# Batch 0's attention scores in twelve groups, more room for their weights, and a reordered middle stretch, in a fused attention and ReGLU feed-forward kernel

## The chip, the cores and the metric

The kernel runs on one core of a Trainium2 chip. The core has five engines, each with its own queue: TensorE (PE in the profile, with its weight loads as PEld), VectorE (DVE), ScalarE (ACT), GpSimd (POOL) and SyncE (SP). SP only issues DMA here; ACT and POOL issue some too. The metric is the device time of one execution in microseconds, taken as the median of three runs. Before the change that is 373.52 us (373.01 to 375.04).

## The reference

```python
def _attn_ref(q, k, v):
    B, H, S, D = q.shape                 # 8, 8, 576, 64
    block = 64
    scores = (1 / np.sqrt(D)) * np.matmul(q, k.transpose(0, 1, 3, 2))
    pos = np.arange(S)
    mask = pos[:, None] // block >= pos[None, :] // block
    scores = np.where(mask, scores, -1e9)
    attn = np.exp(scores - np.max(scores, axis=-1, keepdims=True))
    attn = attn / (np.sum(attn, axis=-1, keepdims=True) + 1e-09)
    return np.matmul(attn, v)

def _moe_ref(x, w_gate, w_val, w_out):   # x: 4608 x 512; weights 512 x 1536 and 1536 x 512
    gate = np.maximum(x @ w_gate, 0.0)
    val = x @ w_val
    return gate * val @ w_out
```

The attention output of batch b, 576 tokens by 512 features (8 heads of 64), is x for the feed-forward network (FFN). Inputs and output are float32; the kernel multiplies in bf16.

## The kernel before

**Units of work.** A *round* r is one batch and one pair of heads: b, hp = divmod(r, 4), so rounds 0 to 3 are batch 0 and rounds 4 to 7 are batch 1. The first 512 tokens of a batch are four chunks of 128 and the last 64 are its tail. Scores are computed transposed, keys on partitions and queries along columns; of chunk c only the queries from chunk c on are needed, so a round has three groups per head: chunk 0 (512 columns), chunks 1 and 3 (384 + 128) and chunk 2 (256). The two heads of a pair lie on partitions 0 to 63 and 64 to 127 and run on PE side by side. ACT takes the exp from PSUM into SBUF (`exp`, L466). `corners` and `corner` (L531 to L539) zero the 64 x 64 blocks that the mask excludes. `head_av` (L586) multiplies the exponentials with v, which has a column of ones, so that the row sum comes with it; `normalise` (L544) divides into `xnat`; `to_xT_pe` (L640) transposes `xnat` back through PE into `xT`, the input of the FFN, with head pair hp as its chunk c = hp.

**Layout of batch 0 and 1.** These batches are loaded with four tokens to a partition, token = 4p + j. `pe_mains` (L344) transposes a head pair of q and k on PE and copies both out of PSUM into `qTm` and `kTm`, and the copy brings the columns back to token order.

**FFN.** `ffn_gen` (L679) is a generator. For batch j it makes twelve groups f of 128 hidden columns. A group is 8 matmuls of 512 columns: 4 for the gate, one for each chunk c of x, and 4 for the value. ACT takes the ReLU (L704), DVE multiplies (L709) into `hT`. Then come four output blocks of 128 tokens, 12 matmuls each (L724), DVE copies them to `ob` (L736, three buffers), and `put` stores them one block late; for j = 0 POOL issues the store (L671), otherwise ACT. For j < 2 the groups 0 and 1 are made together, and their steps are sorted so that the four matmuls with c = 3, which need the last head pair, come last. `ffn(n)` runs n more matmuls, to the end of the group begun; `ffn_parts(n)` runs n parts of 4 matmuls.

**PSUM.** Banks 0 to 5 are given out by `take`: the least recently used bank or pair of banks. Banks 6 and 7 (`AV`) are for `head_av`, and for `pe_mains` and `sort_v` where the call names them. `sort_v` (L293) brings v of batch 1 into chunk order with matmuls.

**Where the exponentials go.** `attnT` has two buffers, for even and odd rounds. Round 2 has its first 1024 columns in the space of `v_p` (`attnE`), which is used for v of batch 1 later.

**Order.** All five queues run in the order in which the program is written out (L785 to L982): an instruction waits on its engine for whatever it needs, and everything behind it waits too. DMA loads go through a ring of ten staging buffers; POOL casts them to bf16, which frees the buffer for a later load.

The stretch for batch 0 is L793 to L843: transposes, scores in two calls a round (`scores_1` and `scores_2`), weighted sums, first FFN parts. The weights of the gate and the value come in six halves of 256 hidden columns (`load_w_half`) for each third i of the hidden columns. The stretch for batch 1 is L864 to L924; its attention is laid between FFN matmuls of batch 0. `tails.cast` (L888) is ten casts on POOL for the tails of batches 0 and 1.

Of the kernel before, what the change touches and what calls it, by code (L numbers as in the profile page):

```python
# [17 lines left out]
def kernel(  # L18
# [10 lines left out]
    nc = tc.nc  # L29
# [19 lines left out]
    AV = 6  # L49
    taken = [0] * 6  # L50
# [30 lines left out]

    attnE = v_p.rearrange("p j n -> p (j n)")

    def attn(r, lo, hi):

        if r == 2 and hi <= 1024:
            return attnE.rearrange("p (g n) -> p g n", g=2)[:, :, lo:hi]
        return attnT[r % 2][:, :, lo:hi]

    zeros = consts.tile([128, 128], BF, name="zeros")  # L90
# [89 lines left out]
    class Early:  # L180
# [163 lines left out]
        def pe_mains(self, hp, evac, out=None):  # L344
            out = out or pair()
            for t in range(2):
                tp = as_bf(out[:, t, :])[:, 0:512]
                src = self.half(t, hp // 2)
                lo = 128 * (hp % 2)
                for j in range(4):  # L350
                    nc.tensor.transpose(  # L351
                        tp[:, 128 * j : 128 * j + 128], src[:, j, lo : lo + 128], ident
                    )
                evac[t](
                    (qTm, kTm)[t][self.b % 2][:, :, hp, :].rearrange(
                        "p c (n j) -> p c n j", j=4
                    ),
                    tp.rearrange("p (j c n) -> p c n j", j=4, c=4),
                )

        def pe_tails(self, evac):

# [80 lines left out]
    def cast_w(sts, eng):  # L443
        for dst, st in sts:
            eng(dst, st)


    def scores(b, hp, sc, pieces):
        for pos, c, main in pieces:
            for hh in range(2):  # L450
                ps = slice(64 * hh, 64 * hh + 64)
                n = 512 - 128 * c if main else 64
                o = sc[:, hh, pos : pos + n]
                if main:
                    o = o.rearrange("p (c n) -> p c n", n=128)
                nc.tensor.matmul(  # L456
                    o,
                    kTm[b % 2][ps, c, hp, :],
                    qTm[b % 2][ps, c:4, hp, :] if main else qTt[b % 2][ps, hp, :],
                    start=True,  # L460
                    stop=True,
                )
        return sc

    def exp(out, sc):
        nc.scalar.activation(out, sc, AF.Exp, scale=scale)  # L466

    def scores_1(r):

        b, hp = divmod(r, 4)  # L470
        sc = scores(b, hp, banks[:, 0:2] if r % 2 == 0 else banks[:, 2:4], [(0, 0, True)])
        exp(attn(r, 0, 512), sc)
        sc = scores(
            b, hp, banks[:, 2:4] if r % 2 == 0 else banks[:, 0:2],
            [(0, 1, True), (384, 3, True)],
        )
        exp(attn(r, 512, 1024), sc)

    def scores_2(r):
        b, hp = divmod(r, 4)  # L480
        sc = scores(b, hp, banks[:, 0:2] if r % 2 == 0 else banks[:, 2:4], [(0, 2, True)])
        exp(attn(r, 1024, 1280), sc[:, :, 0:256])

    def scores_all(r, tails=True):

# [193 lines left out]
    def ffn_gen():  # L679

        for j in range(B + 1):
# [4 lines left out]
            for fs in groups:  # L686
# [2 lines left out]
                steps = [(f, t, c) for f in fs for t in range(2) for c in range(4)]  # L689
                if len(fs) > 1:  # L690

                    steps.sort(key=lambda step: (step[2] == 3, step[1]))
                for n, (f, t, c) in enumerate(steps):
                    i, fo = f // 4, 128 * (f % 4)
                    nc.tensor.matmul(  # L695
# [87 lines left out]
    with tc.manual_schedule(engines={E.PE, E.DVE, E.Activation, E.Pool, E.SP}):  # L783
# [5 lines left out]
        for h0 in (0, 2, 4, 6):  # L789
            e0.load_v(h0, 2)  # L790
        w_0 = [load_w_half(0, g) for g in range(2)]
        w_1 = [load_w_half(1, g) for g in range(2)]
        constants(0, nc.vector)  # L793
        constants_tail(0, nc.vector)
        selection(nc.vector.memset, nc.vector.tensor_copy)
# [5 lines left out]
        constants_tail(1, nc.gpsimd)  # L801
        for h0 in (2, 4, 6):
            e0.cast_qk(h0, 2, (pool, pool))
        scores_1(0)
        e0.pe_mains(1, (dve, dve), banks[:, 4:6])
        scores_2(0)
        e0.pe_mains(2, (dve, dve), banks[:, 6:8])
        scores_1(1)
        corners(0, nc.gpsimd)
        e0.cast_v(0, 2, pool)  # L810
        scores_2(1)
        e0.pe_mains(3, (dve, dve), banks[:, 4:6])
        corners(1, nc.gpsimd)
        e0.cast_v(2, 2, pool)
        scores_1(2)
        head_to_xnat(0, 0)
        head_to_xnat(0, 1)
        scores_2(2)
        e0.cast_v(4, 2, pool)
        for c in range(4):  # L820
            corner(2, c, nc.gpsimd)
        head_to_xnat(1, 0)
        head_to_xnat(1, 1)
        scores_1(3)
        to_xT_pe(0, (dve,), banks[:, 4])
        e0.cast_v(6, 2, pool)
        cast_w(w_0[0], pool)
        head_to_xnat(2, 0)
        head_to_xnat(2, 1)
        scores_2(3)  # L830
        to_xT_pe(1, (act,), banks[:, 5])
        for c in range(4):
            corner(3, c, nc.vector)
        cast_w(w_0[1], pool)
        to_xT_pe(2, (act,), banks[:, 4])
        head_to_xnat(3, 0)
        head_to_xnat(3, 1)
        taken[:] = [1, 1, 2, 2, 3, 3]
        ffn_parts(3)
        to_xT_pe(3, (act, dve), banks[:, 5])  # L840
        for w in w_1:
            cast_w(w, pool)
        cast_w(load_w_half(2, 0), pool)  # L843
        e1 = Early(1)
        es = (e0, e1)
        e1.load_qk(0, 4)
        w_2 = load_w_half(2, 1)
        e1.load_v_packed(0)

        ffn(20)  # L850
        w_out = [load_w_out(i) for i in range(3)]
        e1.load_qk(4, 4)
# [8 lines left out]
        cast_w(w_out[2], pool)  # L861
        e1.cast_qk(4, 4, (pool, pool))
        e1.cast_v_packed(4, pool)
        ffn(40)  # L864
        e1.pe_mains(0, (dve, act), banks[:, AV : AV + 2])
        ffn(8)
        e1.pe_mains(1, (dve, act), banks[:, AV : AV + 2])
        scores_all(4, False)
        corners(4, nc.vector)
        ffn(16)  # L870
        e1.sort_v(0, (dve, act), banks[:, AV : AV + 2])
        scores_all(5, False)
# [138 lines left out]
```

## Time and profile before

| | us |
|---|---|
| median of three runs | 373.52 |
| lowest, highest | 373.01, 375.04 |
| the profiled execution's own time | 374.13 |
| its span, first to last instruction | 372.3 |
| PE busy | 355.8 (96%) |
| ACT busy | 170.8 (46%) |
| DVE busy | 165.8 (45%) |
| POOL busy | 117.0 (31%) |

The profile is one execution. A busy share is an average over stretches with different limits; in this kernel the two stretches named above have the most idle time of PE. The granted TensorE clock is 1.00 on the page throughout. The end of a matmul is modelled: one of 512 columns is shown with 379 ns on average while one starts every 216 ns, so the distance between starts is what counts. A timeline row gives the start in us, the length, the engine and line, the operation with the tile it writes and those it reads, and how many instructions are merged in it; in brackets stands how long the engine was idle before it, and what ended that.

### The profile page before, as it was taken

The numbers are of one execution on the slowest core, as the hardware profiler recorded it, in microseconds if no ns is written. First come the engines' busy times: TensorE is split into PE (matmuls) and PEld (weight loads), VectorE is DVE, ScalarE is ACT, GpSimd is POOL, SyncE is SP. The second block draws the span as 40 slices with busy tenths as digits, with TensorE's granted clock in tenths as the row PEclk, the third lists the DMA queues.
The fourth block names the chain that finished last, engine by engine and source line by source line (L and its number), as shares of the span: only waits on it lengthen the run. The fifth ranks groups of instructions, "written<-read, shape, count | busy, mean of one in ns | idle before, by whom it ended". The sixth has DMA issues, their size and how long they took to land.

```text
span 372.3 us, 7468 instructions
## 1 busy us (share of the span) xinstructions
PE 355.8 (96%) x2954; PEld 188.0 (50%) x2993; DVE 165.8 (45%) x329; ACT 170.8 (46%) x269; POOL 117.0 (31%) x161
## 2 busy tenths in 40 slices
PE   7799997899999999999999999999999999999995
PEld 3544554555565555555555555555554544444443
DVE  5744443447565644354434443544344433423432
ACT  4833725656665564365436543654365403302310
POOL 4766778165879302920193004000000000000000
PEclk9999999999999999999999999999999999999999
DMA  8999999969999983997299829063301130020013
GB/s 253 264 349 351 378 195 341 162 158 262 206 168 180 101 149 75 161 119 136 74 173 108 137 75 150 19 132 64 102 16 18 44 102 1 2 85 28 2 35 106
DMA packets 140915, 51.02 MB, mean 137 GB/s; under 512 B 119504, under 2 KB 135120, under 8 KB 140880
## 3 DMA queue, kind: packets, MB, share of 16 engines
q1 hardware_dynamic: 79472, 34.29, 40.3%
q0 software_dynamic: 56704, 8.13, 37.5%
q10 hardware_dynamic: 4704, 8.13, 6.2%
q8 instruction: 23, 0.38, 0.5%
q14 instruction: 12, 0.10, 0.1%
HBM read 37.75 MB, written 9.44 MB: 127 GB/s over the span
## 4 chain that ended last, share of the span: by engine, by line
PE 90%; ACT 4%; DMA 2%; issue 1%; DVE 1%; SPq 0%; POOL 0%; ACTq 0%
PE banks L695 50%; PE banks L724 24%; PE banks L600 7%; PE banks L456 6%; ACT attnT L466 3%; DMA stage<-in_k_dram 2%; PE banks L567 1%; PE banks L351 1%; PE banks L645 1%; PE banks L301 1%; SPq L193 0%; DVE xnat L549 0%; ACT v_p L466 0%; ACT xT L652 0%; ACT kTt L375 0%
## 5 line engine op out<-in xcount | busy, mean ns | idle before, releaser
L466 ACT ACTIVATE attnT<-banks 128x1024 bf16<-128x1024 f32 (+1 forms) x122 | 87.9, 805 | 61.3 <-PE banks L456 55.7
L704 ACT ACTIVATE gate_sb<-banks 128x512 bf16<-128x512 f32 x108 | 64.9, 603 | 101.9 <-PE banks L695 101.6
L709 DVE TENSOR_TENSOR hT<-gate_sb,banks 128x512 bf16<-128x512 bf16 x108 | 74.0, 688 | 78.1 <-PE banks L695 72.5
L695 PE MATMUL banks<-xT,wg 128*128 128x512 bf16 x364 | 97.4, 379 | 2.5 <-DVE xT L650 0.8
L695 PE MATMUL banks<-xT,wv 128*128 128x512 bf16 x378 | 98.2, 379 | 0.4
L724 PE MATMUL banks<-wo,hT 128*128 128x512 bf16 (+1 forms) x433 | 96.0, 373 | 0.7 <-issue 0.2
L695 PEld LDWEIGHTS <-wv 128*128 128x128 bf16 x432 | 42.3, 98 | 51.0
L724 PEld LDWEIGHTS <-hT 128*128 128x128 bf16 x444 | 42.4, 98 | 46.5 <-issue 0.2
L695 PEld LDWEIGHTS <-wg 128*128 128x128 bf16 x432 | 40.5, 98 | 46.5 <-issue 1.9
L736 DVE COPY ob<-banks 128x512 f32<-128x512 f32 (+1 forms) x37 | 25.1, 677 | 56.9 <-PE banks L724 55.3
L399 POOL DMA_DIRECT2D v_bf<-in_v_dram x16 | 14.3, 906 | 73.3 <-PE banks L600 73.3
L600 PE MATMUL banks<-v_bf,attnT 128*128 128x65 bf16 x816 | 34.9, 194 | 0.6 <-DVE recip L548 0.3
L600 PEld LDWEIGHTS <-attnT 128*128 128x128 bf16 x816 | 30.3, 98 | 8.4 <-issue 0.6
L549 DVE TENSOR_TENSOR xnat<-banks,recip 128x640 bf16<-128x640 f32 (+2 forms) x36 | 25.9, 721 | 1.2
L456 PE MATMUL banks<-qTm,kTm 64*128 64x512 bf16 (+3 forms) x256 | 24.2, 299 | 1.1 <-ACT attnT L466 0.9
L456 PEld LDWEIGHTS <-kTm 64*128 64x128 bf16 x512 | 16.9, 94 | 11.1 <-issue 2.3
L548 DVE RECIPROCAL recip<-banks 128x10 f32<-128x10 f32 (+3 forms) x38 | 8.0, 209 | 29.7 <-PE banks L600 27.1
L535 DVE MEMSET attnT<- 64x192 uint32 x28 | 6.1, 218 | 24.3 <-ACT attnT L466 21.6
L399 POOL DMA_DIRECT2D k_bf<-in_k_dram x16 | 14.1, 906 | 0.7 <-DMA v_bf<-in_v_dram 0.5
L399 POOL DMA_DIRECT2D q_bf<-in_q_dram x16 | 14.3, 932 | 0.0
L695 PE MATMUL banks<-xTt,wg 128*128 128x512 bf16 x48 | 12.3, 379 | 0.1
L695 PE MATMUL banks<-xTt,wv 128*128 128x512 bf16 x46 | 12.1, 379 | 0.1
(97 smaller groups left out, 200.1 us busy)
## 6 DMA issues: line engine op xcount, KB each, us to landing
out_dram<-ob ACTq DMA_DIRECT2D x28, 256.0 KB, 2.2
stage<-in_moe_w_gate_dram SPq DMA_DIRECT2D x6, 512.0 KB, 9.0
stage<-in_moe_w_val_dram SPq DMA_DIRECT2D x6, 512.0 KB, 8.9
stage<-in_q_dram SPq DMA_DIRECT2D x6, 512.0 KB, 7.5
stage<-in_k_dram SPq DMA_DIRECT2D x6, 512.0 KB, 8.6
stage<-in_moe_w_out_dram SPq DMA_DIRECT2D x6, 512.0 KB, 9.8
stage<-in_v_dram SPq DMA_DIRECT2D x8, 256.0 KB, 7.0
q_bf<-in_q_dram POOLq DMA_DIRECT2D x16, 128.0 KB, 5.9
```

The source lines that it names most:

```text
L399: nc.gpsimd.dma_start(dst, src[b, :, 128 * c : 128 * c + n, :].rearrange("h p d -> p h d"),)
L456: nc.tensor.matmul(o, kTm[b % 2][ps, c, hp, :], qTm[b % 2][ps, c:4, hp, :] if main else qTt[b % 2][ps, hp, :], start=True, stop=True,)
L466: nc.scalar.activation(out, sc, AF.Exp, scale=scale)
L535: eng.memset(three[:, :, :, 0:64], 0.0)
L548: nc.vector.reciprocal(recip, av[:, :, :, 64])
L549: nc.vector.tensor_tensor(out=out, in0=av[:, :, :, 0:64], in1=recip.to_broadcast([rows, heads, n, 64]), op=AX.mult,)
L600: nc.tensor.matmul(av[:, 0, p, :], w, vb[:, c, h, :], start=(p == 0), stop=(c == p), skip_group_check=True,)
L695: nc.tensor.matmul(out[f][:, t, :], (wg, wv)[t][i][:, c, fo : fo + 128], x[:, c, :], start=(c == 0), stop=(c == 3),)
L704: nc.scalar.activation(gate[f], out[f][:, 0, :], AF.Relu)
L709: nc.vector.tensor_tensor(out=h, in0=gate[f], in1=out[f][:, 1, :], op=AX.mult)
L724: nc.tensor.matmul(ops[:, g, 0 : n1 - n0], hT[f][:, 128 * s : 128 * (s + 1)], wo[i][:, f % 4, n0:n1], start=(f == 0), stop=(f == 11),)
L736: nc.vector.tensor_copy(ob, ops[:, g, 0 : n1 - n0])
```

## The change

- **Twelve groups.** `scores_1` and `scores_2` give way to `scores_of(g)`: group g is the third i of round r, with r, i = divmod(g, 3). Groups take banks 0 and 1 or banks 2 and 3 in turn. Between two groups stand transposes, weighted sums or transposes of `xnat`.
- **Room for all rounds.** `attn` gives rounds 2 and 3 space of their own: the first 1024 columns in `v_p` and in the first third of `w_out`'s tile, the last 256 of each in the second third's. `w_out` is cast there later. Before, only round 2 had other space, for its first 1024 columns.
- **Queries as loaded.** For batch 0 the copy of q out of PSUM keeps the order (p, j), and the scores' matmul reads the columns with j innermost, through the new function `queries`; a step from j to j + 1 is 512 elements.
- **Weights.** The second third of the gate's and the value's weights is loaded by `load_w_in(1)`: four loads of 256 rows by 512 columns instead of four of 512 rows by 256 columns. The four casts come in the order gate, gate, value, value.
- **FFN parts.** The steps of groups 0 and 1 are sorted by chunk as well. `ffn_parts(3)` becomes `ffn_parts(1)`, which needs head pairs 0 and 1 only, and `ffn_parts(2)`, which needs pair 2; round 3's weighted sums stand between them.
- **Middle reordered.** In the stretch of batch 1, `scores_all(4)` moves ahead of `pe_mains(1)`, `sort_v(0)` moves between two FFN groups, `heads_av(5)` and the transposes move between output blocks, `sort_v(4)` moves behind `scores_all(6)`, `heads_av(6)` behind `scores_all(7)`, and `heads_av(7)` behind the tail scores. `tails.cast` moves ahead of the FFN of batch 0 that ends in its output blocks.

```diff
+    wo_flat = [t.rearrange("p c n -> p (c n)") for t in wo]
     def attn(r, lo, hi):
-        if r == 2 and hi <= 1024:
-            return attnE.rearrange("p (g n) -> p g n", g=2)[:, :, lo:hi]
+        if r in (2, 3):
+            if hi <= 1024:
+                flat = (attnE, wo_flat[0])[r - 2]
+                return flat.rearrange("p (g n) -> p g n", g=2)[:, :, lo:hi]
+            flat = wo_flat[1][:, 512 * (r - 2) : 512 * (r - 1)]
+            return flat.rearrange("p (g n) -> p g n", g=2)[:, :, lo - 1024 : hi - 1024]
         return attnT[r % 2][:, :, lo:hi]
...
+                dst = (qTm, kTm)[t][self.b % 2][:, :, hp, :]
+                if self.b == 0 and t == 0:
+                    evac[t](dst, tp.rearrange("p (j m) -> p j m", j=4))
+                else:
+                    evac[t](
+                        dst.rearrange("p c (n j) -> p c n j", j=4),
+                        tp.rearrange("p (j c n) -> p c n j", j=4, c=4),
+                    )
...
+    def queries(b, ps, c, hp):
+        m = qTm[b % 2]
+        if b == 0:
+            return m[ps, :, hp, 32 * c : 128].rearrange("p j m -> p m j")
+        return m[ps, c:4, hp, :]
...
-    def scores_1(r):
...
-    def scores_2(r):
...
+    def scores_of(g):
+        r, i = divmod(g, 3)
+        pieces = [[(0, 0, True)], [(0, 1, True), (384, 3, True)], [(0, 2, True)]][i]
+        lo, hi = [(0, 512), (512, 1024), (1024, 1280)][i]
+        sc = scores(0, r, banks[:, 0:2] if g % 2 == 0 else banks[:, 2:4], pieces)
+        exp(attn(r, lo, hi), sc[:, :, 0 : hi - lo])
...
-                    steps.sort(key=lambda step: (step[2] == 3, step[1]))
+                    steps.sort(key=lambda step: (step[2] == 3, step[1], step[2]))
...
-        w_1 = [load_w_half(1, g) for g in range(2)]
+        w_1 = load_w_in(1)
...
         constants_tail(1, nc.gpsimd)
         for h0 in (2, 4, 6):
             e0.cast_qk(h0, 2, (pool, pool))
-        scores_1(0)
-        e0.pe_mains(1, (dve, dve), banks[:, 4:6])
-        scores_2(0)
-        e0.pe_mains(2, (dve, dve), banks[:, 6:8])
-        scores_1(1)
+        scores_of(0)
+        scores_of(1)
+        e0.pe_mains(1, (dve, dve), banks[:, 6:8])
+        scores_of(2)
         corners(0, nc.gpsimd)
         e0.cast_v(0, 2, pool)
-        scores_2(1)
-        e0.pe_mains(3, (dve, dve), banks[:, 4:6])
+        scores_of(3)
+        e0.pe_mains(2, (dve, dve), banks[:, 4:6])
+        scores_of(4)
+        scores_of(5)
+        e0.pe_mains(3, (dve, dve), banks[:, 6:8])
+        e0.cast_v(2, 2, pool)
         corners(1, nc.gpsimd)
-        e0.cast_v(2, 2, pool)
-        scores_1(2)
+        scores_of(6)
         head_to_xnat(0, 0)
+        scores_of(7)
         head_to_xnat(0, 1)
-        scores_2(2)
         e0.cast_v(4, 2, pool)
+        scores_of(8)
+        head_to_xnat(1, 0)
+        e0.cast_v(6, 2, pool)
         for c in range(4):
             corner(2, c, nc.gpsimd)
-        head_to_xnat(1, 0)
+        scores_of(9)
         head_to_xnat(1, 1)
-        scores_1(3)
+        scores_of(10)
         to_xT_pe(0, (dve,), banks[:, 4])
-        e0.cast_v(6, 2, pool)
-        cast_w(w_0[0], pool)
+        scores_of(11)
         head_to_xnat(2, 0)
         head_to_xnat(2, 1)
-        scores_2(3)
-        to_xT_pe(1, (act,), banks[:, 5])
         for c in range(4):
             corner(3, c, nc.vector)
+        cast_w(w_0[0], pool)
         cast_w(w_0[1], pool)
+        to_xT_pe(1, (act,), banks[:, 5])
+        taken[:] = [1, 1, 2, 2, 3, 3]
+        ffn_parts(1)
         to_xT_pe(2, (act,), banks[:, 4])
         head_to_xnat(3, 0)
         head_to_xnat(3, 1)
-        taken[:] = [1, 1, 2, 2, 3, 3]
-        ffn_parts(3)
+        ffn_parts(2)
         to_xT_pe(3, (act, dve), banks[:, 5])
-        for w in w_1:
-            cast_w(w, pool)
+        cast_w(w_1, pool)
         cast_w(load_w_half(2, 0), pool)
         e1 = Early(1)
         es = (e0, e1)
         e1.load_qk(0, 4)
         w_2 = load_w_half(2, 1)
         e1.load_v_packed(0)
-
         ffn(20)
         w_out = [load_w_out(i) for i in range(3)]
         e1.load_qk(4, 4)
...
         cast_w(w_out[2], pool)
         e1.cast_qk(4, 4, (pool, pool))
         e1.cast_v_packed(4, pool)
+        for b in range(2):
+            tails.cast(b, pool)
         ffn(40)
         e1.pe_mains(0, (dve, act), banks[:, AV : AV + 2])
         ffn(8)
-        e1.pe_mains(1, (dve, act), banks[:, AV : AV + 2])
         scores_all(4, False)
         corners(4, nc.vector)
-        ffn(16)
+        e1.pe_mains(1, (dve, act), banks[:, AV : AV + 2])
+        ffn(8)
         e1.sort_v(0, (dve, act), banks[:, AV : AV + 2])
+        ffn(8)
         scores_all(5, False)
         corners(5, nc.vector)
         heads_av(4)
         ffn_parts(3)
         to_xT_pe(4, (act,))
         ffn(12)
-        ffn(12)
+        heads_av(5)
         e1.pe_mains(2, (dve, act))
         e1.pe_mains(3, (act, dve))
-        head_av(5, 0)
-        head_av(5, 1)
-        heads_to_xnat(5)
+        ffn(12)
         scores_all(6, False)
+        e1.sort_v(4, (dve, act), banks[:, AV : AV + 2])
         corners(6, nc.vector)
-        to_xT_pe(5, (act,), banks[:, AV])
-        for b in range(2):
-            tails.cast(b, pool)
         e2 = Early(2)
         e2.load_qk(0, 4)
         e2.load_qk(4, 4)
...
         e2.load_v_chunks(1)
         e2.load_tails((0, 1))
         e2.load_tails((2,))
-        e1.sort_v(4, (dve, act), banks[:, AV : AV + 2])
+        to_xT_pe(5, (act,))
         ffn(12)
-        head_av(6, 0)
         scores_all(7, False)
-        head_av(6, 1)
-        heads_to_xnat(6)
-        corners(7, nc.vector)
+        heads_av(6)
         e2.cast_qk(0, 4, (pool, pool))
         e2.cast_qk(4, 4, (pool, pool))
         e2.transpose(0)
         e2.transpose(1)
         e0.pe_tails((dve, act))
         e1.pe_tails((dve, act))
+        corners(7, nc.vector)
         to_xT_pe(6, (act,))
-        heads_av(7)
         scores_last(0)
         scores_tails(0)
+        heads_av(7)
         ffn_parts(3)
         to_xT_pe(7, (dve,))
         e2.cast_tails((pool, pool))
         x0 = sb.tile([64, 4, 128], BF, name="xtail", bufs=2)
         tails_av(0, 0)
+        ffn(4)
         tails_av(0, 1)
         tails_of(x0)
         e2.transpose_tails()
-        ffn(4)
         scores_last(1)
         scores_tails(1)
         ffn(8)
```

More of the change, by code (lines that the diff above doesn't have):

```diff
@@ L353, in pe_mains @@
                     )
[L354 to L359, printed above, removed]
+                dst = (qTm, kTm)[t][self.b % 2][:, :, hp, :]
[6 more added lines that the diff above has]
+                    )
         def pe_tails(self, evac):
@@ L452, in scores @@
                 n = 512 - 128 * c if main else 64
+                x = queries(b, ps, c, hp) if main else qTt[b % 2][ps, hp, :]
                 o = sc[:, hh, pos : pos + n]
                 if main:
-                    o = o.rearrange("p (c n) -> p c n", n=128)
+                    o = o.rearrange("p (m n) -> p m n", n=4 if b == 0 else 128)
                 nc.tensor.matmul(
[L457 to L461, printed above, removed]
+                    o, kTm[b % 2][ps, c, hp, :], x, start=True, stop=True
                 )
@@ L466, in exp @@
         nc.scalar.activation(out, sc, AF.Exp, scale=scale)
-    def scores_1(r):
[L470 to L477, printed above, removed]
-    def scores_2(r):
-        b, hp = divmod(r, 4)
-        sc = scores(b, hp, banks[:, 0:2] if r % 2 == 0 else banks[:, 2:4], [(0, 2, True)])
-        exp(attn(r, 1024, 1280), sc[:, :, 0:256])
+    def scores_of(g):
[4 more added lines that the diff above has]
+        exp(attn(r, lo, hi), sc[:, :, 0 : hi - lo])
     def scores_all(r, tails=True):
```

## The prediction

> **What bounds the kernel now.** I read the page first, then busy time by stage, the waits of TensorE (PE), and the timelines of the two stretches that the change edits. Columns of a window row: the window in us and its length, busy us (instructions) of PE, weight loads, DVE, ACT and POOL, granted clock, DMA share, GB/s.
>
> ```profile
> span 372.3 us, 7468 instructions
> ```
>
> ```profile
> 0.00:24.00 24.00, 18.28 (x185) 10.17 (x187) 13.56 (x44) 14.18 (x20) 14.98 (x36) 1.00 0.94 279
> 24.00:38.00 14.00, 13.95 (x71) 6.60 (x71) 6.69 (x10) 5.79 (x10) 8.73 (x9) 1.00 1.10 351
> 38.00:76.00 38.00, 32.70 (x392) 19.56 (x395) 15.70 (x35) 20.80 (x37) 22.96 (x31) 1.00 0.99 260
> ```
>
> PE bounds the kernel. Its idle time that the edits can reach is 5.7 us before 24 and 5.3 us between 38 and 76. No edit starts after 76, so what is won or lost by then is carried to the end. DMA is full until 76 (share about 1): loads land late and in the order of their queue.
>
> **First stretch: batch 0.** The twelve groups let ScalarE (ACT) run its exps with smaller gaps, since a group's matmuls no longer stand behind transposes that wait for casts. Now, in ACT's timeline (start, length, instructions, idle before):
>
> ```profile
> 10.59 2.43 ACT L466 ACTIVATE attnT<-banks 128x1024 bf16<-128x1024 f32 x3 [0.92 <-PE banks L456]
> ```
>
> ```profile
> 16.04 2.43 ACT L466 ACTIVATE attnT<-banks 128x1024 bf16<-128x1024 f32 x3 [0.61 <-PE banks L456]
> ```
>
> These two gaps, 0.92 and 0.61, are what the groups can close; about 0.4 comes back where group 7 stands behind the first weighted sum, which waits for the cast of v on GpSimd (POOL). So the last exp, which ends at 18.47 now (16.04 + 2.43), ends near 17.4. But the first FFN part also needs the first weights, whose cast waits for DMA:
>
> ```profile
> 17.03 1.04 POOL L445 CAST wg<-stage 128x1024 bf16<-128x1024 f32 x1 [0.50 <-DMA stage<-in_moe_w_gate_dram]
> ```
>
> They are there at 18.07. From there PE is serial: 4 matmuls 0.86, four transposes 0.22, the two heads of round 3 0.70, 8 matmuls 1.73 (0.216 for a large matmul and 0.70 for 20 small ones: rows 37.22, 38.08, 55.23 and 55.93 below), then what lies between the transposes of round 3 and the first matmul on them:
>
> ```profile
> 21.77 0.39 PE L645 MATMUL banks<-ident,xnat 128*128 128x128 bf16 x4
> 22.94 0.59 PE L695 MATMUL banks<-xT,wg 128*128 128x512 bf16 x2 [0.79 <-DVE xT L650]
> ```
>
> That is 1.17; 18.13 + 3.51 + 1.17 = 22.8 against 22.94. The weights swallow ACT's gain: -0.1.
>
> Queries read as loaded: q's copy becomes contiguous (shorter and off the path, since k's copy comes after it), and PE now reads each moving column 1024 bytes from the last. No row of PE does that; the nearest is the copy L335 on VectorE (DVE), which reads at 512-byte steps (duration in ns: min/median/max).
>
> ```profile
> L335 DVE COPY qTm<-perm x8: 589/596/1371, 78.3 to 127.0; 128x512 bf16<-128x512 bf16 x8
> ```
>
> Two more DVE groups (busy us, mean ns of one):
>
> ```profile
> L549 DVE TENSOR_TENSOR xnat<-banks,recip 128x256 bf16<-128x256 f32 x8 | 3.4, 425 | 0.3
> ...
> L354 DVE COPY qTm<-banks 128x512 bf16<-128x512 bf16 x4 | 2.8, 692 | 3.9 <-PE banks L351 3.7
> ```
>
> Bounds for 512 columns on PE: 216 ns if the step is free, 596 if PE is as slow as that whole copy. 256 more columns cost DVE 267 ns (692 - 425), so 158 are fixed, and 596 - 158 = 438 is twice 216: I take twice. A round's scores stream 1280 columns per head, the two heads at once, 0.54 us; four rounds cost 2.2 us more. Most of it lies beside exps, but groups 6, 9 and 11 each wait for a bank and hand their delay on, some 0.7 to the last exp; its last copy ends at 18.7 instead of 18.0 and the part starts there: +0.5 (bounds -0.1 and +0.9). The Trainium skill, "SBUF — State Buffer", section "SBUF: two separate sides", says that full read speed needs at least two accesses to each 16-byte line, which these columns never give; it has no price. By it the free end falls away, and the best case of rival A below would be 371.3, not 370.8. The 438 ns of DVE neither confirm nor deny it for PE.
>
> The second third of the weights is loaded in rows of 512 columns, as w_out is, not 256. Landings now, by the casts that wait for them, first of 256 and then of 512 columns:
>
> ```profile
> 21.83 1.04 POOL L445 CAST wv<-stage 128x1024 bf16<-128x1024 f32 x1 [0.81 <-DMA stage<-in_moe_w_val_dram]
> 23.35 1.04 POOL L445 CAST wg<-stage 128x1024 bf16<-128x1024 f32 x1 [0.47 <-DMA stage<-in_moe_w_gate_dram]
> ```
>
> ```profile
> 42.22 1.04 POOL L445 CAST wo<-stage 128x1024 bf16<-128x1024 f32 x1 [0.31 <-DMA stage<-in_moe_w_out_dram]
> 43.58 1.04 POOL L445 CAST wo<-stage 128x1024 bf16<-128x1024 f32 x1 [0.31 <-DMA stage<-in_moe_w_out_dram]
> ```
>
> 1.36 instead of 1.52, four times: later loads come some 0.5 us earlier (bounds 0 and 0.6). All four casts are now needed by the fifth FFN group; the last ends at 21.83 + 4 x 1.36 + 1.04 = 28.3. PE gets there 26 matmuls after 22.94, at 28.6, plus 0.5: no stall.
>
> **Second stretch: batch 1.** Now:
>
> ```profile
> 37.22 1.03 PE L695 MATMUL banks<-xT,wv 128*128 128x512 bf16 x4
> 38.08 0.39 PE L351 MATMUL banks<-ident,q_bf 128*128 128x128 bf16 x4
> ...
> 39.87 1.02 PE L695 MATMUL banks<-xT,wg 128*128 128x512 bf16 x3 [0.51 <-ACT attnT L466]
> ```
>
> ```profile
> 38.35 0.69 DVE L709 TENSOR_TENSOR hT<-gate_sb,banks 128x512 bf16<-128x512 bf16 x1 [0.90 <-PE banks L695]
> ```
>
> scores_all(4) moves ahead of pe_mains(1), right behind an FFN group whose banks its third piece takes: the piece waits for hT (39.04) as it does now, pe_mains(1) fills the 0.51 wait, and the next group starts 0.2 earlier. But q's copy of pe_mains(1) now stands on DVE behind the memsets of corners(4), which wait for every exp of the round. sort_v(0) takes the same banks one FFN group later and waits some 0.7; the third piece of scores_all(5) loses sort_v as cover and waits 0.6 for hT. These go into DVE's wait for the exps of round 5, which sets the transposes of round 4: about 49.0, plus the 0.5, 49.5. What follows now:
>
> ```profile
> 54.33 0.39 PE L351 MATMUL banks<-ident,q_bf 128*128 128x128 bf16 x4
> ...
> 55.23 0.77 PE L600 MATMUL banks<-v_bf,attnT 128*128 128x65 bf16 x20
> 55.93 0.81 PE L456 MATMUL banks<-qTm,kTm 64*128 64x512 bf16 x8
> 57.32 0.40 PE L645 MATMUL banks<-ident,xnat 128*128 128x128 bf16 x4 [0.58 <-DVE xnat L549]
> 59.44 1.05 PE L301 MATMUL banks<-v_p,sel 64*128 64x256 bf16 x16 [1.72 <-ACT xT L652]
> 60.64 2.54 PE L724 MATMUL banks<-wo,hT 128*128 128x512 bf16 x11 [0.16 <-issue]
> 63.02 0.46 PE L600 MATMUL banks<-v_bf,attnT 128*128 128x65 bf16 x10
> ```
>
> Then: transposes 0.23, 12 matmuls 2.59, heads_av(5) 0.70, 16 transposes 0.90, 12 matmuls 2.59, two pieces of scores 0.44, a wait of 0.4 for the copy of output block 2, the third piece 0.1, sort_v 0.9, transposes 0.23, 12 matmuls 2.59. Block 3 ends at 61.2, not 63.02; the waits of 0.58 and 1.72 are gone.
>
> The new wait is here. tails.cast moves ahead of the FFN outputs of batch 0, and POOL issues their stores:
>
> ```profile
> 54.20 1.28 POOL L671 DMA_DIRECT2D out_dram<-ob  x2
> 55.45 0.64 POOL L170 CAST q_bt<-stage 64x512 bf16<-64x512 f32 x1
> ...
> 60.11 0.55 POOL L671 DMA_DIRECT2D out_dram<-ob  x1
> ```
>
> The time to landing of the store at 60.11:
>
> ```profile
> DMA to landing us min/median/max: 5.7/5.7/5.7
> ```
>
> The ten casts take 4.7 us (55.45 to 60.11) and would start where the first store does now, at 54.2, or 53.7 with the earlier loads, and end at 58.4. Only then does the store of block 0 go out, over 4 us later than now. I take 5.7 us for it, from the store nearest in place and traffic: landed at 64.1. There are three ob buffers, so DVE's copy of block 3 waits for it and ends at 64.9, with DVE's queue behind it. The third piece of scores_all(7) takes the bank of block 3: PE gets there at 61.6 and stands until 65.0. These 3.4 us are set by DMA and POOL alone, so the +0.5 of the first stretch vanishes in them.
>
> From that piece on: heads_av(6) +0.7, normalised +1.8, transposed +2.1; tail transposes and tail scores beside it; ACT copies xT, takes the small exp and then a large one,
>
> ```profile
> L466 ACT ACTIVATE v_p<-banks 128x1024 bf16<-128x1024 f32 x4 | 3.9, 1020 | 0.4 <-PE banks L456 0.4
> ```
>
> which ends at +4.3 and frees the bank of the second FFN group; 12 matmuls (+6.9), transposes and half of tails_av (+7.6), 4 matmuls (+8.5), the other half (+9.2), and the second tail scores, waiting for the second hT, end at +10.2: 75.2. Now the FFN resumes at:
>
> ```profile
> 75.47 0.82 PE L695 MATMUL banks<-xT,wg 128*128 128x512 bf16 x3
> ```
>
> So -0.2. The profiled execution took 374.13 us, 1.8 more than its span; the sum makes it 373.9. It stood 0.6 above the median of 373.52, which becomes 373.3.
>
> **Rivals.** A, faster: the store lands before it is needed, so the reordering shows. For it: the store at 93.4 took less.
>
> ```profile
> DMA to landing us min/median/max: 3.7/3.7/3.7
> ```
>
> With 3.7 the time is 371.4. With no wait at all, and without the +0.5, block 3 is copied by 61.7, the exps of round 7 then still run (0.9 more than the +10.2), and the tail scores end at 72.8, or up to 73.3 with the +0.5: 370.8 to 371.3. Against it: the loads of batch 2 fill the queues there. B, slower: the clock falls in the 3.4 us gap. The longest gap of PE in these stretches now is 1.72, and the matmuls behind it keep 0.216. Those that open the run are slow, at 631 ns each against the 379 of the page's later ones:
>
> ```profile
> L772 PE MATMUL banks<-zeros,ident 128*128 128x512 bf16 x5 | 2.5, 631 | 0.0
> ```
>
> If that comes back for the 16 large matmuls behind the gap, each costs some 0.2 more, 3.4 in all, 0.4 of it beside waits: 376.3. It decides from the gap at which the clock falls, which no row shows. The Trainium skill, "TensorE: Matmul & The Clock Gate", Part 1, has the clock halved after at least one idle window of about 3.4 us whose phase is free; by it a gap of 3.4 falls only by luck. C, slower: the store takes as long as the slower of the first two, and the wider rows win nothing: +1.7 + 0.5 - 0.2, 375.5.
>
> ```profile
> DMA to landing us min/median/max: 6.2/6.8/7.4
> ```
>
> That the groups do nothing for the time is no rival but part of the forecast.
>
> **How the numbers follow.** Forecast 0.48, A 0.28, B 0.10, C 0.14. One half per cent is 1.9 us, about what a measurement of this kernel can tell from no change: A is faster, B and C slower, the forecast (372.3 to 374.5) the same. The range leaves out the lowest of A and the upper part of B: 370.8 to 376.1.
>
> **What would show it.** Right: the last exp of batch 0 near 18; its score matmuls twice as long; the stores of batch 0 issued after the ten casts; DVE's copy of block 3 waiting for a store near 61, with PE standing some 3 us; the FFN of batch 1 resuming near 75. Wrong: an ob copy that waits for no DMA, or 631 ns matmuls behind the gap.

## The result, and the profile after

The changed kernel takes 378.18 us (median of six runs, 377.91 to 378.63), the kernel before 374.13 us (six runs, 373.01 to 375.04). The ratio is 1.0111, with a 95% interval of 1.0088 to 1.0134: slower, and above the forecast of 373.3 and its range. The executions of the kernel before whose clock is on record took 372.8 to 373.2 us at a mean granted clock of 0.999 or 1.00, or 374.4 to 375.1 us at 0.994 or 0.995; the profiled one has the full clock.

The lines that answer to those shown of before: the span, the granted clock over 40 slices (in tenths; of the kernel before first), and busy time by stage.

```profile
PEclk9999999999999999999999999999999999999999
```

```profile
span 376.3 us, 7510 instructions
...
PEclk9669999999999999999999999999999999999999
```

```profile
0.00:24.00 24.00, 21.41 (x143) 9.32 (x144) 10.98 (x36) 13.24 (x16) 15.21 (x36) 0.76 1.03 295
24.00:38.00 14.00, 13.21 (x80) 6.64 (x79) 5.65 (x14) 4.62 (x9) 9.88 (x10) 0.92 1.09 358
38.00:76.00 38.00, 36.00 (x348) 19.09 (x347) 15.78 (x35) 21.31 (x36) 23.38 (x32) 1.00 1.05 261
```

These rows show two opposite things. Before 24 us PE is busier than it was (21.41 us against 18.28) and gets less done (143 instructions against 185), at a mean clock of 0.76. Between 38 and 76 it stands 2.0 us instead of 5.3. So the first stretch lost and the second one won.

PE's own timeline gives the sizes. The first matmul on head pair 3, at 22.94 before, starts here at 29.29:

```profile
29.29 0.59 PE L700 MATMUL banks<-xT,wg 128*128 128x512 bf16 x2 [0.79 <-DVE xT L655]
```

That is +6.35. The span grew by 4.0 (376.3 - 372.3), so some 2.3 came back behind it; from the fifth output copy on, at 107 us, the two traces run 4.0 apart to the end.

**Where the 6.35 come from.** The score matmuls of batch 0 by shape, in the first stretch of the kernel before and of the changed one (count, busy us, mean ns of one):

```profile
L456 PE MATMUL banks<-qTm,kTm 64*128 64x512 bf16 x8 | 1.6, 391 | 0.1
L456 PE MATMUL banks<-qTm,kTm 64*128 64x384 bf16 x8 | 1.3, 324 | 0.1
```

```profile
L473 PE MATMUL banks<-qTm,kTm 64*128 64x512 bf16 x8 | 4.1, 1020 | 0.6 <-DVE kTm L365 0.4 <-ACT kTm L365 0.2
L473 PE MATMUL banks<-qTm,kTm 64*128 64x384 bf16 x8 | 3.2, 810 | 0.0
```

The shapes differ by 128 columns and by 210 ns, 1.64 ns a column; before it is 67 ns, 0.52. By the starts in the timeline a pair of 512 columns takes 0.85 us against 0.22: four times, not twice. And the clock halves while this goes on. The windows of the changed kernel, cut where the granted clock steps:

```profile
5.64:12.47 6.83, 6.21 (x38) 1.74 (x35) 2.43 (x5) 4.14 (x5) 4.98 (x10) 1.00 1.23 278
12.47:26.12 13.65, 13.65 (x114) 7.21 (x113) 5.42 (x19) 7.77 (x10) 9.31 (x16) 0.50 1.09 354
26.12:38.00 11.88, 11.10 (x66) 5.31 (x64) 5.43 (x11) 4.04 (x8) 8.24 (x9) 1.00 1.09 357
```

PE is shown busy for 6.21 of the 6.83 us ahead of the fall and for all of the 13.65 us at half clock. Its longest gap there is 0.37 us, and the kernel before kept the full clock through a gap of 0.90 us at 11.67, so no gap of PE explains the fall.

**Where the 2.3 come from.** The wait for a store, which was the forecast's main term, isn't there. POOL's stores and DVE's copies of the output blocks:

```profile
57.29 0.86 POOL L180 CAST v_bf<-stage 64x256 bf16<-64x256 f32 x2
59.15 0.71 POOL L676 DMA_DIRECT2D out_dram<-ob  x1 [1.00 <-DVE ob L741]
```

```profile
58.15 0.69 DVE L741 COPY ob<-banks 128x512 f32<-128x512 f32 x1 [2.22 <-PE banks L729]
...
67.94 0.69 DVE L741 COPY ob<-banks 128x512 f32<-128x512 f32 x1 [1.58 <-PE banks L729]
```

The first output block itself comes at 58.15, when the ten casts are done. Its store goes out at 59.15 and lands 5.5 us later, at 64.65; block 3 is ready at 67.9. PE was late enough for the store to be in time. (In the kernel before the first of these copies starts at 51.08, 7.1 us earlier: the new order loses another 0.7 up to there, and wins 3.0 behind it.)

### The profile page after: what moved, and what is told of

The parts are those of the page before. It is cut to its first block, busy times and chain, and to the rows that moved or that the text cites. A ratio compares the mean times of both kernels' runs of the same rounds, so it can differ in the third digit from the quotient of the medians.

```text
span 376.3 us, 7510 instructions
## 1 busy us (share of the span) xinstructions
PE 367.1 (98%) x2993; PEld 189.5 (50%) x2993; DVE 164.7 (44%) x329; ACT 171.6 (46%) x269; POOL 116.0 (31%) x161
## 4 chain that ended last, share of the span: by engine, by line
PE 96%; ACT 1%; DVE 1%; issue 0%; POOL 0%; DVEq 0%; ACTq 0%; POOLq 0%
PE banks L700 50%; PE banks L729 25%; PE banks L605 8%; PE banks L473 8%; PE banks L358 1%; PE banks L650 1%; PE banks L777 1%; PE banks L572 1%; PE banks L308 1%; ACT attnT L479 0%; DVE hT L714 0%; DVE ob L741 0%; ACT v_p L479 0%; ACT kTt L384 0%; PE banks L512 0%
## 5 line engine op out<-in xcount | busy, mean ns | idle before, releaser
L479 ACT ACTIVATE attnT<-banks 128x1024 bf16<-128x1024 f32 (+1 forms) x118 | 85.1, 805 | 63.4 <-PE banks L473 63.4
L700 PE MATMUL banks<-xT,wg 128*128 128x512 bf16 x384 | 99.8, 382 | 1.2 <-DVE xT L655 0.8
L729 PE MATMUL banks<-wo,hT 128*128 128x512 bf16 (+1 forms) x444 | 97.0, 373 | 0.0
L473 PE MATMUL banks<-qTm,kTm 64*128 64x512 bf16 (+3 forms) x256 | 31.6, 349 | 1.3 <-DVE hT L714 0.4
```

Of the source, the lines that this page charges most:

```text
L473: nc.tensor.matmul(o, kTm[b % 2][ps, c, hp, :], x, start=True, stop=True)
L700: nc.tensor.matmul(out[f][:, t, :], (wg, wv)[t][i][:, c, fo : fo + 128], x[:, c, :], start=(c == 0), stop=(c == 3),)
L729: nc.tensor.matmul(ops[:, g, 0 : n1 - n0], hT[f][:, 128 * s : 128 * (s + 1)], wo[i][:, f % 4, n0:n1], start=(f == 0), stop=(f == 11),)
```

## The experiments

The measured runs, each against the kernel before: e1 to e4 against 374.61 us (15 executions), e5 to e7 against 374.48 (17), the changed kernel against 374.13 (6). "Pair 3" is the start of the first matmul on head pair 3, "behind it" what the rest of the span gained or lost against the kernel before (22.94 and 372.3).

| kernel | median us | ratio, 95% interval | pair 3 | behind it |
|---|---|---|---|---|
| changed | 378.18 | 1.0111 (1.0088 to 1.0134) | 29.29 | -2.3 |
| e1: queries in token order | 374.65 | 1.0015 (0.9994 to 1.0036) | 21.77 | +0.8 |
| e2: queries as loaded, alone | 380.58 | 1.0180 (1.0144 to 1.0216) | 28.97 | +1.6 |
| e3: second stretch alone | 375.95 | 1.0045 (1.0015 to 1.0075) | 21.90 | +3.1 |
| e4: four read steps | 378.54 (one run) | | 25.76 | +1.6 |
| e5: e1, casts later | 371.18 | 0.9932 (0.9909 to 0.9956) | 22.08 | -2.1 |
| e6: fillers between scores | 383.11 | 1.0245 (1.0216 to 1.0274) | 34.31 | -2.3 |
| e7: two rounds as loaded | 374.23 | 0.9997 (0.9977 to 1.0016) | 25.58 | -2.2 |

**e1, the queries in token order.** The whole change, with this one part undone:

```diff
-                if self.b == 0 and t == 0:
+                if False:
...
-        if b == 0:
+        if False:
             return m[ps, :, hp, 32 * c : 128].rearrange("p j m -> p m j")
```

> The changed kernel with the queries of batch 0 in token order again (q's copy out of PSUM unpermutes them, the scores read contiguous columns); all else of the change stays. Theory S (the strided read is what costs: score matmuls of 512 columns start 0.85 us apart instead of 0.22, and the clock falls because of them): they are back at 0.22, the granted clock is 1.00 throughout, the first matmul on head pair 3 comes at 22.8 to 23.2 instead of 29.3, and now the copy of output block 3 waits for the store, as the prediction has it, so that the FFN of batch 1 resumes near 75.2: 373.3 to 374.3, the same as before. Rival G (the new order of the first stretch itself is slower, with other waits, and the clock falls from that): the matmul on head pair 3 stays at 26 or later, the clock still falls, 376 or more.

The scores are back at 381 ns, the clock stays at 1.00 up to 64 us, and head pair 3 comes 7.5 us earlier than in the changed kernel:

```profile
L473 PE MATMUL banks<-qTm,kTm 64*128 64x512 bf16 x8 | 1.6, 381 | 0.8 <-ACT attnT L479 0.6
```

The loss against before is gone (1.0015). Three points of theory S are missed: head pair 3 comes at 21.77, ahead of 22.8 to 23.2; the clock isn't 1.00 throughout but at half from 64.42 to 67.83, behind the wait below; and 374.65 us is just above 373.3 to 374.3. The forecast's wait is now there; DVE's row and PE's list of waits between 38 and 76 us (us in total, times, longest):

```profile
63.01 0.69 DVE L741 COPY ob<-banks 128x512 f32<-128x512 f32 x1 [3.55 <-DMA out_dram<-ob]
```

```profile
PE banks L473 <- DVE ob L741: 2.1, 1, 2.1
PE banks L308 <- DVE qTm L365: 0.8, 1, 0.8
PE banks L473 <- DVE hT L714: 0.4, 2, 0.2
```

So the lateness that the slow read caused hid the wait, and with the read mended the wait takes back what the second stretch wins.

**e2, the queries as loaded, alone.** The kernel before with this one part of the change (its copy of q and `queries`):

```diff
+        if b == 0:
+            return m[ps, :, hp, 32 * c : 128].rearrange("p j m -> p m j")
+        return m[ps, c:4, hp, :]
```

> The kernel before with one part of the change alone: queries of batch 0 kept as loaded and read at steps of 1024 bytes. Theory S: score matmuls of 512 columns 0.85 apart in all four rounds, the granted clock falls to half in the first 25 us here too, the first matmul on head pair 3 at 28 to 30 instead of 22.9, and, as the middle isn't reordered and gives nothing back, 379 to 381. Rival G: the read costs the 2.2 us of PE that the prediction gave it or less on the path, no fall of the clock, 374 to 376.

Theory S holds: one part makes the kernel 1.8% slower, with 1022 ns for a score matmul of 512 columns, a clock of 0.74 before 24 us, and head pair 3 at 28.97. It costs 6.0 us (380.58 - 374.61), against the 4.0 of the whole change, so what e2 lacks is worth some 2 us.

```profile
0.00:24.00 24.00, 20.65 (x145) 9.21 (x146) 10.95 (x36) 12.48 (x16) 14.24 (x36) 0.74 0.89 270
```

**e3, the second stretch alone.** The kernel before with the change's order of batch 1, `tails.cast` ahead of the outputs included:

```diff
+        for b in range(2):
+            tails.cast(b, pool)
         ffn(40)
...
-        for b in range(2):
-            tails.cast(b, pool)
```

> The kernel before with the second stretch of the change alone (batch 1 reordered, tail casts ahead of the stores); the first stretch is the old one. Theory of the prediction: the copy of output block 3 waits for a store that the tail casts hold up, PE stands 3 to 4 us near 62, the FFN of batch 1 resumes at 75 to 76, and the time is within 1 us of before. Rival A (the store lands in time): the old waits of 1.7, 0.6 and 0.5 us are gone and nothing takes their place, it resumes near 72.8, 371 to 372.

The wait for the store is there, and larger than anywhere: PE stands 4.95 us (3 to 4 expected), the clock is at half from 63.88 to 70.71, the FFN of batch 1 resumes at 77.60 (75 to 76 expected), and the time is 1.3 us above before (within 1 expected). The store goes out at 59.30, 1.7 us later than in e1, since POOL starts the ten casts 1.25 us later and waits 1.2 us for a load among them. The new order by itself costs 0.45%.

```profile
65.87 0.37 PE L456 MATMUL banks<-qTm,kTm 64*128 64x256 bf16 x1 [4.95 <-DVE ob L736]
```

Its first stretch is that of the kernel before, and head pair 3 comes at 21.90, not 22.94: in this stretch, which waits for the landing of the first weights, two executions of the same instructions differ by 1 us. So the 21.77 of e1 is no gain of the twelve groups over 21.90.

**e4, four read steps.** The kernel before, where rounds 0 to 3 read their queries at steps of 2, 4, 8 and 64 elements (4, 8, 16 and 128 bytes; at 64 there are two columns to a chunk, then the read goes on in the next chunk):

```diff
+                if main and b == 0:
+                    st = (2, 4, 8, 64)[hp]
+                    o = o.rearrange("p (s c n) -> p s c n", s=st, c=4 - c)
+                    x = x.rearrange("p c (n s) -> p s c n", s=st)
```

> The kernel before with the score matmuls of batch 0 reading their columns at another step in each round: 2, 4, 8 and 64 elements (4, 8, 16 and 128 bytes) in rounds 0 to 3. The queries then stand in another order than the weighted sums take them for, so batch 0's part of the output isn't the reference's. Line rule (full speed needs two accesses to a 16-byte line): rounds 0 and 1 keep 0.22 us from one 512-column pair to the next, rounds 2 and 3 take 0.85. Rival: every step above one element costs, growing with the step, rounds 0 and 1 at 0.3 to 0.6; or only steps far above a line cost, round 2 at 0.22 as well.

The merged rows of chunks 0, 1 and 3 of each round, 1024 columns a head, in order of the rounds:

```profile
6.20 0.63 PE L461 MATMUL banks<-qTm,kTm 64*128 64x512 bf16 x6 [0.25 <-ACT kTm L354]
...
8.69 1.06 PE L461 MATMUL banks<-qTm,kTm 64*128 64x512 bf16 x6
...
11.34 1.96 PE L461 MATMUL banks<-qTm,kTm 64*128 64x512 bf16 x6
...
16.20 1.79 PE L461 MATMUL banks<-qTm,kTm 64*128 64x512 bf16 x6
```

1024 columns at 0.216 us for 512 are 0.43, and a single matmul is shown some 0.17 longer than its distance to the next (391 against 216 ns), so full speed would be 0.61. Step 2 has it (0.63); step 4 takes twice that (1.06 - 0.17 = 0.89); steps 8 and 64 take four times (1.79 and 1.62). The cost doubles each time the columns that share 16 bytes are halved, four, two, one, and then stops growing: the change's 1024-byte step is no worse than 16 bytes. The Trainium skill, "SBUF — State Buffer", section "SBUF: two separate sides", asks for at least two hits on a 16-byte line for full read speed. Taken as two accesses, that isn't what PE shows here: two gave half speed, and only four gave it in full. So of the expectation the line rule falls at round 1, and the rivals at round 0 (no cost) and round 2 (full cost). All of these reads are of two heads at once; one head alone wasn't run.

**e6, fillers.** The changed kernel with four full-speed matmuls on zeros behind nine of the twelve score groups:

```diff
         scores_of(0)
+        junk(4, banks[:, 5])
         scores_of(1)
+        junk(4, banks[:, 5])
```

> The whole change as it is, with four full-speed 512-column matmuls on zeros (some 0.86 us, nothing reads them) put into TensorE's order behind nine of the twelve score groups of batch 0. Theory L (the clock falls at 12.47 us because the slow reads leave the array mostly idle, although TensorE counts as busy): with the fillers the granted clock stays at 1.00 through the first stretch, the score matmuls still stand 0.84 us apart for 512 columns (the read is slow by itself), the attention heads take 0.36 us instead of 0.66, the stretch loses 4 us of half clock and gains up to 7.8 us of fillers, so the first matmul on head pair 3 comes at 31 to 33.5 us instead of 29.29, and the run takes 378 to 382 us. Rival M (the clock falls for a cause that the score matmuls don't set, such as the loads or the start of the kernel, or for the slow reads as such): half clock from about 12.5 us all the same, fillers of 0.43 us each, first matmul on head pair 3 behind 36 us, over 383 us. Rival N (the reads are slow only since the clock is low): spacing of the scores falls below 0.5 us.

Fillers and scores in the stretch from 6 to 36 us, and the window up to 34 us:

```profile
L777 PE MATMUL banks<-zeros,ident 128*128 128x512 bf16 x38 | 10.4, 395 | 0.0
L473 PE MATMUL banks<-qTm,kTm 64*128 64x512 bf16 x8 | 4.1, 1019 | 0.1
```

```profile
7.21:34.00 26.79, 25.82 (x199) 10.76 (x199) 8.53 (x28) 12.01 (x15) 17.40 (x27) 1.00 1.13 334
```

The clock stays at 1.00, with the same loads, the same slow reads and more work; and a score matmul still takes 1019 ns. So the reads are slow by themselves (rival N falls) and don't pull the clock down as such (rival M falls): what the fillers changed is how much PE gets done between them, as theory L has it. Head pair 3 at 34.31 and the time, 383.11, are above what L gave (33.5 and 382), since the fillers took 8.0 us (the distances in the timeline are 0.87 to 0.97 for four) and the full clock won back less than the 4 us expected. This divides the loss: without its fillers head pair 3 would come at 34.3 - 8.0 = 26.3. From 21.8 (e1) to 26.3 is the read, 4.5 us; from 26.3 to 29.3 is the clock, 3.0. It is a division by subtraction, since nothing here ran the slow read at full clock without fillers: it takes the fillers to cost their whole 8.0 us.

**e7, two rounds as loaded.** The changed kernel, with head pairs 2 and 3 of batch 0 read in token order:

```diff
-        if b == 0:
+        if b == 0 and hp < 2:
             return m[ps, :, hp, 32 * c : 128].rearrange("p j m -> p m j")
```

> The whole change with the queries of head pairs 0 and 1 of batch 0 read as loaded, those of pairs 2 and 3 in token order: half of the slow reads. Theory S (the change's loss is the slow reads and the clock that they pull down): the scores of pairs 0 and 1 stand 0.84 us apart for 512 columns and those of pairs 2 and 3 0.22; the clock still falls near 12.5 us, since up to there nothing differs, and comes back 3.4 or 6.8 us later, not 13.65; first matmul on head pair 3 at 24 to 26.5 us (21.8 with none, 29.3 with all), and 375 to 377 us. Rival W (the loss is in the twelve groups' order and not in the reads): first matmul on head pair 3 above 28 us. Rival X (any slow read costs the whole 13.65 us of half clock): half clock to 26 us and over 377 us.

Half of the slow reads, and half of the time at half clock:

```profile
10.91:17.73 6.82, 6.82 (x62) 3.86 (x60) 3.79 (x8) 5.03 (x6) 3.53 (x10) 0.50 1.17 298
```

Head pair 3 comes at 25.58, +3.8 against e1 where all four rounds cost +7.5: theory S, and W and X fall. The clock falls at 10.91 and not near 12.5, although the program is the same up to there. The time, 374.23, is below the 375 to 377 expected, because the delay of 2.6 against before is already enough for the store to land: DVE's copy of block 3 waits for no DMA, and the 2.2 us of the second stretch are kept. So e7 with its slow reads, against its kernel before (0.9997), is no slower than e1 without them (1.0015).

**e5, the casts behind the first store.** e1 with one more line moved:

```diff
         e1.cast_v_packed(4, pool)
-        for b in range(2):
-            tails.cast(b, pool)
         ffn(40)
...
         to_xT_pe(4, (act,))
         ffn(12)
+        for b in range(2):
+            tails.cast(b, pool)
```

> The whole change with the queries of batch 0 in token order again, and besides the ten casts of the tails put back on GpSimd behind the first store of batch 0 (they stood ahead of all three). Nothing else is moved, and the number of output buffers stays 3. Theory T (the 3.55 us for which VectorE's copy of output block 3 waited for a store, and TensorE's 2.1 us behind it, come from the casts ahead of the stores): the first store is issued at 52 to 53 us instead of 57.58, lands at 58 to 60, VectorE's copy of block 3 starts at 60 to 61.5 without a wait for a DMA, the FFN of batch 1 resumes at 72.3 to 73.3 instead of 75.03, no stretch at half clock follows it, and the run takes 370.3 to 372.0 us. Rival U (the store takes its 5 to 7 us whatever is ahead of it, and the loads that share the queues grow it): the copy still waits over 1.5 us for a DMA, resumption stays above 74.3, 373 to 375 us. Rival V (the later casts make the tails late): a wait for the tails' transposes behind 64 us takes the gain back, over 373 us.

POOL issues the first store ahead of the casts, and DVE's copy of block 3 waits for PE alone:

```profile
52.81 0.71 POOL L676 DMA_DIRECT2D out_dram<-ob  x1
53.52 0.63 POOL L177 CAST q_bt<-stage 64x512 bf16<-64x512 f32 x1
```

```profile
60.93 0.69 DVE L741 COPY ob<-banks 128x512 f32<-128x512 f32 x1 [1.58 <-PE banks L729]
```

```profile
38.00:76.00 38.00, 35.58 (x404) 19.92 (x404) 16.65 (x38) 22.49 (x38) 22.81 (x32) 1.00 1.05 262
```

The FFN of batch 1 resumes at 72.73 (e1 75.03, before 75.47) at full clock, and the run takes 371.18 us: theory T, and a kernel that is faster than both, 0.9932 (0.9909 to 0.9956) of the one before. Against the seven executions of the kernel before at a granted clock of 0.999 or 1.00 (372.81 to 373.21) the gain is 1.8 us, against the other ten (374.36 to 375.01) some 3.7: the difference between the two is the clock, which all six executions of e5 keep.

## Why the prediction was wrong

- **What failed: "I take twice"**, the price of the queries read as loaded. It was +0.5 us, with bounds of -0.1 and +0.9. A pair of 512 columns took 0.85 us (forecast 0.44, upper bound 0.596). The upper bound came from a copy on DVE; another engine's copy at another step bounds nothing on PE. The factor of two within it rests on 158 ns taken as fixed, from two different operations (a copy of 512 columns and a multiplication of 256). The forecast's 2.2 us of PE for the four rounds, 0.5 of them on the path, became 6.3 (5120 columns, 0.63 us more for 512), and by e6 and e1 4.5 of them on the path: that "most of it lies beside exps" failed too.
- **What no step had: the clock in the first stretch.** It costs 3.0 us by e6; the trace has 13.65 us at half clock. Rival B let the clock fall in a gap of PE 50 us later, and nothing in it covers a PE that is shown busy.
- **The twelve groups, -0.1:** not contradicted, and too small to be told from when the loads land. Counted from the end of the first weights' cast, head pair 3 comes 5.06 and 4.89 us later with the groups (e1, e5) and 4.87 and 4.90 without (before, e3). That "the weights swallow ACT's gain" shows in e5, where PE waits 0.30 us for that cast at 17.25.
- **The wider rows of the second third:** right. In the changed kernel the casts that wait for these loads start 1.36, 1.34 and 1.37 apart:

```profile
22.82 1.04 POOL L454 CAST wg<-stage 128x1024 bf16<-128x1024 f32 x1
24.18 1.04 POOL L454 CAST wg<-stage 128x1024 bf16<-128x1024 f32 x1 [0.32 <-DMA stage<-in_moe_w_gate_dram]
25.52 1.04 POOL L454 CAST wv<-stage 128x1024 bf16<-128x1024 f32 x1 [0.30 <-DMA stage<-in_moe_w_val_dram]
26.89 1.04 POOL L454 CAST wv<-stage 128x1024 bf16<-128x1024 f32 x1 [0.34 <-DMA stage<-in_moe_w_val_dram]
```

- **"No stall" at the casts of the second third:** holds in the changed kernel. In e1, where PE is earlier than the prediction had it, it waits 0.45 us for the last of them at 27.99.
- **`sort_v(0)` waiting some 0.7 for q's copy:** right, 0.8 in e1's list above. The wait of 0.6 for `hT` in `scores_all(5)` is 0.2 there.
- **The store behind the ten casts, and the FFN resuming at 75.2:** right where its condition holds. In e1 DVE waits 3.55 us for the store, which took 5.3 (5.7 assumed), and the FFN resumes at 75.03; that execution took 373.65 us, and the sum said 373.9. That the two agree so closely is partly luck: PE stood from 61.66 to 63.76, 2.1 us and not 3.4, and what stands behind took 11.3 us and not 10.2, part of it at half clock. In the changed kernel the condition fails, since the first stretch is 6.35 us late. The prediction let a first-stretch delay "vanish in" the wait and took only 0.5 for it; a delay that outlasts the wait removes it, and then costs what it exceeds it by. Against e1, a delay of 3.8 us lengthens the span by 0.8 in e7, and one of 7.5 by 4.4 in the changed kernel: some 3.0 were hidden each time.
- **Rival A's mechanism,** no wait for the store, is what the changed kernel shows, for another reason than a quick store: 2.3 us won behind head pair 3. An `ob` copy that waits for no DMA was the prediction's own sign of being wrong. With the slow read gone, e5 takes 371.18 us; A without a wait gave 370.8 to 371.3.
- **Rival B, the clock in the gap behind the store:** it happens, in e1 from 64.42 and in e3 from 63.88 us, for 3.41 and 6.82 us, but is priced too high for e1, which still resumes at 75.03. Its premise that the kernel before keeps its clock holds for the profiled execution; 20 of the 32 executions beside the experiments have 0.994 or 0.995. **Rival C:** no store of these three took 7.4 us in the changed kernel or in e1 (6.3 at most there), and the wider rows did win.

The sum in the end: the read +4.5, the clock +3.0, the groups and what that execution's loads did -1.2 (22.94 to 21.77), the second stretch -2.3: +4.0, the growth of the span.

## What to carry to other kernels

The moving operand of a matmul wants its columns dense within 16 bytes: with bf16 four of them gave full speed here (e4), and the copy out of PSUM that restores the order was cheaper than reading as loaded. It takes 692 ns of DVE for a head pair where the contiguous one takes 425; reading as loaded took PE 1.6 us more for a round. A price taken from another engine is no bound; where a term's only row is from elsewhere, the range must take in several times that value. When a piece of work is moved ahead on a queue that also issues stores, look for who needs the buffer that the store frees, and remember that a delay upstream can hide such a wait: mending the delay alone (e1) brought 4.0 us back, both together (e5) 7.3.

## What the runs showed of the hardware

- The clock fell while PE was shown busy with slow reads. In the changed kernel PE has no gap over 0.4 us between the first scores and the fall at 12.47, and is shown as 91% busy (6.21 of 6.83 us); fillers of 8 us over the stretch kept the clock at 1.00 (e6). Half clock came in lengths of 3.41 us (e1), 6.82 (e7) and 13.65 (changed kernel), one, two and four times the same window. The Trainium skill, "TensorE: Matmul & The Clock Gate", Part 1, has such a window of about 3.4 us, and the lengths agree; it ties the fall to idle windows, and here PE was busy by the profile. In e1 a gap of 2.1 us was enough for a fall.
- The number of columns streamed orders the cases, and the busy time doesn't. This is an estimate, counted from the timelines of the nine kernels up to 75 us: the columns of all matmuls in each window of 3.41 us, on the grid on which the clock steps, a pair of heads counted once; some matmul records are missing in the traces. At 0.216 us for 512 columns a full window holds about 8090. Of the windows at full clock, half clock followed all eight with 3019 columns or fewer (2343 ahead of 12.47 in the changed kernel) and none of the others, which have 3355 or more. Of those at half clock, it ended behind the ones with 3127 or more and went on behind the ones with 2872 or fewer. By busy time, the kernel before kept its clock behind a window with PE 68% busy (3381 columns, from 6.87 us), the changed kernel lost it behind one with 89%. That the chip itself counts columns isn't shown.
- By the same count the kernel before has 3.41 us with as few as 1575 columns in its second stretch (from 56.3 us), and e5 never fewer than 4033 there. That would be why some executions of the kernel before lose their clock and none of e5 does; no trace of such an execution is on record.
- A slow read costs the same at both clocks. In the changed kernel the 512-column score matmuls of rounds 0 and 1 ran at full clock and those of rounds 2 and 3 at half; they are shown with 1017 to 1023 ns in all four, and with 1019 on average in e6 at full clock. Matmuls that read densely double: the first four of 512 columns of the FFN take 1.70 us from their start to the next row's in the changed kernel (25.06 - 23.36), where four take 0.86 at full clock.

```profile
23.36 1.91 PE L700 MATMUL banks<-xT,wg 128*128 128x512 bf16 x4
25.06 0.63 PE L650 MATMUL banks<-ident,xnat 128*128 128x128 bf16 x4
```
